# Linear attention into a bilinear feed-forward layer: an out product in three parts, sums moved and cut, a bank and a state copy moved

## The chip, the cores and the metric

One core of a Trainium2 chip runs the whole program in one launch. The metric is the device time of one execution in microseconds. It was 225.81 us before the change (median of 3 runs, 225.62 to 226.88).

## What is computed

Attention with a decay per head, in blocks with a running state, and then a bilinear feed-forward layer on its output:

```
for b in range(nb):                       # blocks along the sequence, S = 768
    intra = (q_b k_b^T * lam^(i-j), i >= j) v_b
    inter = (q_b * lam^(i+1)) kv_state
    out_b = intra + inter
    kv_state = lam^block * kv_state + (k_b * lam^(block-1-j))^T v_b
x   = out, heads side by side             # 3072 tokens x 512
out = ((x @ w_a) * (x @ w_b)) @ w_out     # d_ff = 1536, float32 in and out
```

There are 4 batches, 8 heads of 64 columns and 768 positions.

## The kernel before

The 3072 tokens are 24 units of 128 tokens, six to each batch. Eight groups of units, `GROUPS = (4, 1, 2, 4, 4, 4, 4, 1)`, go through the feed-forward layer one after the other, so unit 4 is group 1, units 5 and 6 are group 2, units 7 to 10 group 3, units 19 to 22 group 6 and unit 23 group 7.

TensorE always has the feed-forward layer of one group as its main work. The attention of later units is put between its matmuls by hand: the layer calls `hook(slot)` at numbered places, and `PLAN[group]` says which pieces stand at which slot. Each engine runs its own instructions in the order in which the program issues them. The pieces that matter here:

- `P u` (`PK` and `PV`): scale the keys and queries (GpSimd, line L401) and cast the values of unit u. From unit 7 on SP then starts a DMA that transposes keys and queries into `qkT` (L429); for units 4 to 6, `T u` does it on TensorE and ScalarE copies the result (L445).
- `S u`: the scores of unit u (TensorE, `kq`, L457) and their masks (`m`, VectorE, L480, for some units with a ScalarE copy ahead).
- `O2 (u, w)`: the outputs of two units (`o_ps`, L497), head half by head half; each half is copied by ScalarE into the transposed tile `xT` (L520) that the feed-forward layer reads. `V u` adds to the running state (`kvd`, L527) and copies it to `st`; `KV_ENG` says whether VectorE does this in one instruction (L560) or ScalarE in two (L558).
- `WS i`: one of eight sums of weight blocks, `wz_a` and `wz_b` (L269 to L275), by the engine in `WS_ENG`.
- `X g`: sums of `xT` for group g: `z_sub`, `z_add`, `z_mix` (L706 to L708).

Groups 0, 1, 2 and 7 go through `ffn`: for each of 12 column blocks `a_ps` (L596, copied by ScalarE, L605), `b_ps`, and their product `ab` (VectorE, L623); then the out product `op` (L643) and its copy by ScalarE (L634 or L638). For group 1 the out product has two halves of six matmuls, with slot 12 (`S 6`) between them and slot 13 (`P 8`, the outputs of units 5 and 6, `V 6`, both weight sums) behind them.

Groups 3 to 6 go through `ffn_z`, in which seven smaller products over sums of x and of weights stand for eight blocks. For each of 6 steps these go into banks called U, V and W (L731); ScalarE copies two of them out as `u` (L812) and VectorE subtracts those (`oab`, L760 to L777). The last product of a step waits for this and is issued in the next step; ScalarE then copies U (L737) and VectorE multiplies (L739). In the first step of group 3, which is not joined with an earlier group's out product, the order is: `xT` (U), first half of `z_sub` (V), first column half of `z_add` (W), `z_mix` (U), second column half of `z_add` (V), `xT` again (U); the second half of `z_sub` is read by the last product. The out products of groups 4 to 6 (L853) stand between the products of the following group; they too work with sums, of `ab` (`SM`), by VectorE or GpSimd.

PSUM has 7 banks in rotation. `ps_bank` hands out the next one that is not held; `z_bank` names U, V and W's banks itself. Before group 7 the last product of group 6 is issued into bank 1, and the rotation goes on from where it stood.

Of the kernel before, what the change touches and what calls it, by code (L numbers as in the profile page):

```python
# [17 lines left out]
BF16 = mybir.dt.bfloat16  # L18
# [4 lines left out]
def _bc(ap, dims):  # L23
# [58 lines left out]
Z_GROUPS = (3, 4, 5, 6)  # L82
# [10 lines left out]
                        [0] +  # L93
                        [1] +
                        [0] * 2))
KV_ENG = dict(enumerate(["dve"] * 10 + ["act"] * 2 + ["dve"] + ["act"] * 11))
VB_ENG = dict(enumerate(["pool"] * 7 +
                        ["dve"] * 3 +
                        ["pool"] * 5 +
# [5 lines left out]
                        ["act"] * 3))  # L105
SUM_ENG = {(3, 0): 'dve', (3, 1): 'dve', (3, 2): 'pool', (3, 3): 'dve', (3, 4): 'pool', (3, 5): 'pool', (3, 6): 'dve', (3, 7): 'dve', (4, 0): 'dve', (4, 1): 'pool', (4, 2): 'pool', (4, 3): 'pool', (4, 4): 'dve', (4, 5): 'pool', (4, 6): 'pool', (4, 7): 'pool', (5, 0): 'dve', (5, 1): 'dve', (5, 2): 'pool', (5, 3): 'pool', (5, 4): 'dve', (5, 5): 'pool', (5, 6): 'pool', (5, 7): 'dve', (6, 0): 'pool', (6, 1): 'dve', (6, 2): 'pool', (6, 3): 'dve', (6, 4): 'dve', (6, 5): 'pool', (6, 6): 'dve', (6, 7): 'dve'}
XS_ENG = {(3, 0): 'dve', (3, 1): 'dve', (3, 2): 'dve', (4, 0): 'dve', (4, 1): 'dve', (4, 2): 'dve', (5, 0): 'dve', (5, 1): 'pool', (5, 2): 'pool', (6, 0): 'pool', (6, 1): 'pool', (6, 2): 'pool'}
WS_ENG = {0: 'dve', 1: 'dve', 2: 'dve', 3: 'dve', 4: 'dve', 5: 'dve', 6: 'dve', 7: 'pool'}
WO_ENG = {0: 'dve', 1: 'dve', 2: 'pool', 3: 'dve', 4: 'dve'}
CO_ENG = {0: 'pool', 1: 'pool', 2: 'pool', 3: 'dve', 4: 'dve', 5: 'dve'}  # L110

# [2 lines left out]
def kernel(  # L114
# [11 lines left out]
    nc = tc.nc  # L126
    B, H, S, D = q.shape
# [3 lines left out]
    d_model, d_ff = moe_w_a.shape  # L131
# [4 lines left out]
    FC = d_ff // 128  # L136
# [10 lines left out]
    xz_pool = ctx.enter_context(tc.tile_pool(name="xz", bufs=4))  # L147
# [11 lines left out]
    bank = {"next": 0, "held": set(), "ffn": None}  # L159
# [169 lines left out]
    gx, xTs = {}, {}  # L329
# [67 lines left out]
    def eng_of(name):  # L397
        return nc.gpsimd if name == "pool" else nc.vector
# [232 lines left out]
    def store(row, op, lo, hi, queue=None):  # L631
        if row < g_u0[KEEP_GROUPS]:
            o_sb = snap_pool.tile([128, d_model], F32, name="o_kept", tag="snap")
            nc.scalar.copy(o_sb, op)  # L634
            kept.append((row, o_sb))
            return
        o_sb = o_pool.tile([128, d_model], F32, name="o_sb", tag="osb")
        nc.scalar.copy(o_sb[:, lo:hi], op[:, lo:hi])  # L638
        (queue or nc.sync).dma_start(out=out_r[row][:, lo:hi], in_=o_sb[:, lo:hi])

    def out_mms(op, ab, t, fs, lo=0, hi=d_model):
        for f in fs:
            nc.tensor.matmul(op[:, lo:hi], lhsT=ab[:, f, t * 128:(t + 1) * 128],  # L643
                             rhs=wo_sb[:, f, lo:hi], start=(f == 0), stop=(f == FC - 1))

    def ffn(u0, n, xT, hook, first, last):
        gt = n * BLK
        ab = ab_pool.tile([128, FC, 512], BF16, name="ab", tag="ab")
        if first:
            for i, cs in enumerate(W_STEPS):  # L650
                nxt = W_STEPS[i + 1] if i + 1 < len(W_STEPS) else ()
                fs = range(w_off[cs[0]] // 128, w_off[cs[-1] + 1] // 128)
                a_sbs = a_parts(fs[:2], xT, gt) if i == 0 else []
                a_sbs += [a_part(f, xT, gt) for f in fs[len(a_sbs):]]
                if i == 0:
                    kv_update(n0 - 1)
                    cast_w("b", cs[1], "both")
                else:
                    for c in nxt:
                        cast_w("a", c, "dve")  # L660
                for n_f, (f, a_sb) in enumerate(zip(fs, a_sbs)):
                    b_part(f, xT, gt, a_sb, ab)
                    hook(f)
                    if i == 0 and n_f == 1:
                        cast_w("a", nxt[0], "dve")
                for c in nxt:
                    cast_w("b", c, "act")
            ops = [ps_bank("op", [128, d_model], F32, hold=True) for _ in range(n)]
            slot = FC
            for c in range(FC // 2):  # L670
                for t in range(n):
                    out_mms(ops[t], ab, t, range(2 * c, 2 * c + 2))
                    if c == FC // 2 - 1:
                        store(u0 + t, ops[t], 0, d_model)
                    hook(slot)
                    slot += 1
            bank["held"].clear()
            return
        for f in range(FC):
            a_sb = a_part(f, xT, gt)  # L680
            b_part(f, xT, gt, a_sb, ab)
            hook(f)
        for t in range(n):
            op = ps_bank("op", [128, d_model], F32, ffn=True)
            if last and t == n - 1:
                for lo, hi in ((0, 256), (256, 384), (384, 512)):
                    if lo:
                        op = ps_bank("op", [128, d_model], F32, ffn=True)
                    out_mms(op, ab, t, range(FC), lo, hi)
                    store(u0 + t, op, lo, hi, nc.scalar if hi == d_model else None)  # L690
                return
            out_mms(op, ab, t, range(FC // 2))
            hook(FC + 2 * t)
            out_mms(op, ab, t, range(FC // 2, FC))
            store(u0 + t, op, 0, d_model)
            hook(FC + 2 * t + 1)


    xz = {}

    def x_sums(g):
        xT = gx[g]
        z_add = xz_pool.tile([128, 2, 512], BF16, name="z_add", tag="xz")
        z_sub = xz_pool.tile([128, KS, 256], BF16, name="z_sub", tag="xz")
        z_mix = mix_pool.tile([128, 2, 256], BF16, name="z_mix", tag="z_mix")
        eng_of(XS_ENG[g, 0]).tensor_sub(z_sub, xT[:, :, 0:256], xT[:, :, 256:512])  # L706
        eng_of(XS_ENG[g, 1]).tensor_add(z_add, xT[:, 0:2, :], xT[:, 2:4, :])
        eng_of(XS_ENG[g, 2]).tensor_add(z_mix, xT[:, 0:2, 0:256], xT[:, 2:4, 256:512])  # L708
        xz[g] = (z_add, z_sub, z_mix)

    fin = []
    pairs = [0]
# [285 lines left out]
    for g, n in enumerate(GROUPS):  # L998
        if g + 1 < len(GROUPS):
            new_xT(g + 1)  # L1000
        plan = {}
        for slot, name, us in PLAN.get(g, ()):
            plan.setdefault(slot, []).append((name, us))

        def hook(slot, plan=plan):
            for name, us in plan.get(slot, ()):
                if name == "C":
                    cast_w("o", us, CO_ENG[us])
                elif name == "PK":
                    prep_k(us)  # L1010
                elif name == "PV":
                    prep_v(us)
                elif name == "P":
                    prep_k(us)
                    prep_v(us)
                elif name == "W":
                    store_kept()
                elif name == "WS":
                    weight_sum(us)
                elif name == "WO":  # L1020
                    out_sum(us)
                elif name == "SM":
                    ab_sum(*us)
                elif name == "H":
                    out_half(*us)
                elif name == "X":
                    x_sums(us)
                elif name == "T":
                    piece_T(us)
                elif name == "S":  # L1030
                    piece_S(us)
                elif name == "VC":
                    kv_copy(us, kv["ps"], KV_ENG[us])
                elif name == "V":
                    piece_V(us)
                elif name == "O":
                    pieces_O((us,))
                elif name == "O2":
                    pieces_O(us)
                else:  # L1040
                    pieces_O(us[:2], us[2:])

        if g in Z_GROUPS:
            bank["held"] = set(range(5))
            joined = any(name == "H" and us[0] < g for slot, name, us in PLAN[g])
            own = any(slot >= 18 for slot, name, us in PLAN[g])
            ffn_z(g, g_u0[g], gx.pop(g), hook, joined, own)
        else:
            bank["held"] = {3, 4} if fin else set()
            if fin:  # L1050
                fin.pop()()
            ffn(g_u0[g], n, gx.pop(g), hook, g == 0, g + 1 == len(GROUPS))

# [28 lines left out]
```

## Time and profile before

| | |
|---|---|
| median of 3 runs | 225.81 us (225.62 to 226.88) |
| profiled execution | 225.77 us, of which 224.0 us are the span of the profile |
| TensorE busy | 213.6 us, 95% of the span |
| VectorE, ScalarE, GpSimd busy | 163.5, 123.4, 100.2 us |
| granted TensorE clock | 0.999 of full speed |

In a row of the timeline stand the start and the time taken in microseconds, the engine, the line, the operation, what is written and read, the shape and how many instructions are merged in the row; in brackets the idle time of the engine ahead of it and what ended it. PE is TensorE, PEld its weight loads, DVE VectorE, ACT ScalarE, POOL GpSimd, SP the engine that issues most DMAs. Some matmul records are missing, so a row that says x5 can stand for six. A matmul's end is modelled; its start is recorded.

### The profile page before, as it was taken

What the parts mean: (1) busy time and instruction counts of PE and PEld (TensorE: products, weight loads), DVE (VectorE), ACT (ScalarE), POOL (GpSimd) and SP (SyncE); (2) the same over time, 40 slices, a digit from 0 to 9 for tenths busy, and PEclk for the clock granted to TensorE, in tenths of its full rate; (3) what the DMA queues carried; (4) which work ended last, traced back from release to release, by engine and by line L of the source; (5) the groups of instructions that cost most, each with busy time, mean ns of one, the idle gap of its engine ahead of it and who ended that gap; (6) DMA issues with size and microseconds to landing.
All of it is one profiled execution on the core that took longest, in us unless ns stands there. A gap on an engine that the chain in (4) does not pass through costs nothing.

```text
span 224.0 us, 5599 instructions
## 1 busy us (share of the span) xinstructions
PE 213.6 (95%) x2225; PEld 159.0 (71%) x2235; DVE 163.5 (73%) x269; ACT 123.4 (55%) x251; POOL 100.2 (45%) x95
## 2 busy tenths in 40 slices
PE   7797999999999998999999999899999999999994
PEld 2374444448778756887547888688888888888994
DVE  0994763988798659889977979968686765776440
ACT  2684556018554156675366988776536665533322
POOL 6061004346794076542249369786427722052000
PEclk9999999999999999999999999999999999999999
DMA  4999999999999999999999999752021100112042
GB/s 128 322 253 349 357 387 340 272 221 208 218 187 220 233 188 245 190 281 231 154 247 219 224 220 230 145 94 50 0 96 47 51 0 4 47 52 91 0 143 94
DMA packets 99081, 39.42 MB, mean 176 GB/s; under 512 B 85488, under 2 KB 95088, under 8 KB 99056
## 3 DMA queue, kind: packets, MB, share of 16 engines
q1 hardware_dynamic: 98768, 39.00, 79.2%
q8 instruction: 17, 0.28, 0.6%
q10 hardware_dynamic: 288, 0.07, 0.1%
q14 instruction: 8, 0.07, 0.1%
HBM read 28.32 MB, written 6.29 MB: 154 GB/s over the span
## 4 chain that ended last, share of the span: by engine, by line
PE 86%; DMA 5%; SPq 3%; ACT 2%; DVE 2%; issue 1%; ACTq 0%
PE U L731 18%; PE op L853 12%; PE b_ps L596 10%; PE a_ps L596 9%; PE V L731 9%; PE op L643 9%; PE W L731 5%; PE op L793 5%; PE o_ps L497 4%; DMA wst<-in_moe_w_a_dram 3%; PE kq L457 3%; SPq L187 2%; DMA q<-in_q_dram 2%; PE kvd L527 1%; ACT xT L520 1%
## 5 line engine op out<-in xcount | busy, mean ns | idle before, releaser
L812 ACT COPY u<-U 128x512 f32<-128x512 f32 x48 | 28.4, 591 | 16.4 <-PE U L731 16.2
L401 POOL TENSOR_TENSOR qk<-kf,lp_k 128x512 bf16<-128x512 f32 x18 | 20.7, 1148 | 35.2 <-DMA kf<-in_k_dram 22.1
L623 DVE TENSOR_TENSOR ab<-a_sb,b_ps 128x128 bf16<-128x128 bf16 (+2 forms) x48 | 19.3, 417 | 16.4 <-PE b_ps L596 7.8
L596 PE MATMUL a_ps<-xT,wa_sb 128*128 128x128 bf16 (+2 forms) x198 | 27.6, 267 | 1.6 <-DVE wa_sb L244 1.3
L480 DVE TENSOR_TENSOR m<-kq,lotri 128x512 bf16<-128x512 f32 x40 | 25.7, 683 | 4.2 <-PE kq L457 4.2
L596 PE MATMUL b_ps<-xT,wb_sb 128*128 128x128 bf16 (+2 forms) x192 | 27.5, 272 | 0.5 <-ACT oab L737 0.5
L739 DVE TENSOR_TENSOR ab<-oab 128x1024 bf16<-128x1024 bf16 x24 | 18.4, 766 | 11.7 <-ACT oab L737 11.6
L605 ACT CAST a_sb<-a_ps 128x128 bf16<-128x128 f32 (+2 forms) x48 | 17.3, 375 | 16.7 <-PE a_ps L596 14.8
L401 POOL TENSOR_TENSOR qk<-qf,lp_q 128x512 bf16<-128x512 f32 x20 | 24.5, 1227 | 1.9 <-DMA qf<-in_q_dram 1.9
L643 PE MATMUL op<-wo_sb,ab 128*128 128x512 bf16 (+2 forms) x114 | 21.8, 334 | 0.5 <-issue 0.3
L596 PEld LDWEIGHTS <-wa_sb 128*128 128x128 bf16 x200 | 16.7, 98 | 7.7 <-DVE wa_sb L244 1.5
L731 PEld LDWEIGHTS <-wz_a 128*128 128x128 bf16 x192 | 18.2, 98 | 3.6 <-issue 0.5
L596 PEld LDWEIGHTS <-wb_sb 128*128 128x128 bf16 x192 | 15.7, 98 | 6.6 <-issue 0.6
L731 PEld LDWEIGHTS <-wz_b 128*128 128x128 bf16 x192 | 18.8, 98 | 2.2
L731 PE MATMUL U<-xT,wz_a 128*128 128x256 bf16 x96 | 18.3, 272 | 0.0
L731 PE MATMUL U<-xT,wz_b 128*128 128x256 bf16 x96 | 18.3, 272 | 0.0
L520 ACT CAST xT<-o_ps 128x512 bf16<-128x512 f32 (+1 forms) x24 | 12.2, 556 | 10.7 <-PE o_ps L497 10.5
L731 PEld LDWEIGHTS <-wa_sb 128*128 128x128 bf16 x144 | 13.4, 98 | 4.7 <-issue 2.0
L770 DVE TENSOR_TENSOR oab<-U,u 128x512 bf16<-128x512 f32 x24 | 16.4, 682 | 0.4 <-PE U L731 0.4
L643 PEld LDWEIGHTS <-ab 128*128 128x128 bf16 x120 | 10.2, 98 | 8.5
L737 ACT CAST oab<-U 128x512 bf16<-128x512 f32 x24 | 14.2, 591 | 3.5 <-PE U L731 3.5
L420 POOL CAST vb<-vf 128x512 bf16<-128x512 f32 x14 | 9.7, 695 | 13.4 <-DMA vf<-in_v_dram 12.5
(126 smaller groups left out, 451.9 us busy)
## 6 DMA issues: line engine op xcount, KB each, us to landing
vf<-in_v_dram SPq DMA_DIRECT2D x24, 256.0 KB, 5.1
qf<-in_q_dram SPq DMA_DIRECT2D x20, 256.0 KB, 4.5
kf<-in_k_dram SPq DMA_DIRECT2D x20, 256.0 KB, 4.7
out_dram<-o_sb SPq DMA_DIRECT2D x18, 256.0 KB, 2.4
wst<-in_moe_w_a_dram SPq DMA_DIRECT2D x6, 512.0 KB, 8.6
wst<-in_moe_w_b_dram SPq DMA_DIRECT2D x6, 512.0 KB, 9.1
wst<-in_moe_w_out_dram SPq DMA_DIRECT2D x6, 512.0 KB, 10.6
out_dram<-o_kept SPq DMA_DIRECT2D x5, 256.0 KB, 4.3
```

Of the source, the lines that this page charges most:

```text
L401: eng_of(eng).tensor_mul(dst.rearrange("p (c b) d -> p b c d", b=2), x[:].rearrange("p (b c) d -> p b c d", b=2), lp.rearrange("p (b c) o ...
L480: nc.vector.tensor_mul(m, kq[i], lotri_bc)
L520: nc.scalar.copy(dst, src)
L596: nc.tensor.matmul(ps[:, lo:hi], lhsT=w_sb[:, s, f * 128:(f + 1) * 128], rhs=xT[:, s, lo:hi], start=(s == 0), stop=(s == KS - 1), skip_gro ...
L605: nc.scalar.copy(a_sb[:, :gt], ps[:, :gt])
L623: nc.vector.tensor_mul(ab[:, f, :gt], a_sb[:, :gt], ps[:, :gt])
L643: nc.tensor.matmul(op[:, lo:hi], lhsT=ab[:, f, t * 128:(t + 1) * 128], rhs=wo_sb[:, f, lo:hi], start=(f == 0), stop=(f == FC - 1))
L731: nc.tensor.matmul(ps[:, k, :], lhsT=wt[:, s, n * 128:(n + 1) * 128], rhs=rhs[i][:, s, :], start=(fresh and k == 0 and s == 0), stop=True, ...
L739: nc.vector.tensor_mul(ab[:].rearrange("p (h i) (t c) -> p h i t c", h=2, t=2)[:, :, n], o5[:, :, :, 0, :], o5[:, :, :, 1, :])
L770: nc.vector.tensor_sub(oab[:, 1], U, v1)
L812: nc.scalar.copy(t, ps)
L853: nc.tensor.matmul(ps[:, t, :], lhsT=lhs[p][:, n, t * 128:(t + 1) * 128], rhs=rhs[:, n, :], start=fresh, stop=True, skip_group_check=True)
```

## The change

Five edits. Unit 4's out product is issued in three parts of four matmuls: slot 12 stands behind the first, slot 13 (with the outputs of units 5 and 6 and the state) behind the second, and the third part and the copy of `op` behind these. The last two weight sums move from slot 13 of group 1 to slots 7 and 9 of group 2, and sum 7 goes from GpSimd to VectorE. The sums of x for group 3 are cut from three instructions into five of 128 x 512, in the order in which the products read them; the first of them, over the first two units' columns, is issued ahead of the outputs of units 9 and 10. The state copy of unit 22 goes from ScalarE (two instructions) to VectorE (one). Group 7's rotation of banks starts at bank 5.

```diff
     1: [...
-        (11, 'S', 5), (11, 'T', 6), (12, 'S', 6), (13, 'P', 8), (13, 'O2', (5, 6)), (13, 'V', 6),
-        (13, 'WS', 6), (13, 'WS', 7)],
+        (11, 'S', 5), (11, 'T', 6), (12, 'S', 6), (13, 'P', 8), (13, 'O2', (5, 6)), (13, 'V', 6)],
     2: [(2, 'W', None), (2, 'W', None), (3, 'P', 9), (4, 'V', 7), (4, 'S', 7),
-        (6, 'V', 8), (10, 'PK', 10), (11, 'PV', 10), (11, 'P', 11), (11, 'W', None),
+        (6, 'V', 8), (7, 'WS', 6), (9, 'WS', 7), (10, 'PK', 10), (11, 'PV', 10), (11, 'P', 11), (11, 'W', None),
         (11, 'S', 8), (11, 'P', 12), (12, 'Q', (7, 8, 9, 10)), (13, 'P', 13),
-        (13, 'W', None), (13, 'V', 9), (14, 'O2', (9, 10)), (14, 'X', 3), (15, 'W', None)],
+        (13, 'W', None), (13, 'V', 9), (14, 'XA', 3), (14, 'O2', (9, 10)), (14, 'X', 3), (15, 'W', None)],
...
-KV_ENG = dict(enumerate(["dve"] * 10 + ["act"] * 2 + ["dve"] + ["act"] * 11))
+KV_ENG = dict(enumerate(["dve"] * 10 + ["act"] * 2 + ["dve"] + ["act"] * 9 + ["dve", "act"]))
...
-WS_ENG = {..., 7: 'pool'}
+WS_ENG = {..., 7: 'dve'}
...
+            if n == 1:
+                out_mms(op, ab, t, range(4))
+                hook(FC)
+                out_mms(op, ab, t, range(4, 8))
+                hook(FC + 1)
+                out_mms(op, ab, t, range(8, FC))
+                store(u0 + t, op, 0, d_model)
+                return
...
+    def x_add_first(g):
+        x_first[g] = x_tile()
+        nc.vector.tensor_add(x_first[g][:, :, 0:256], gx[g][:, 0:2, 0:256], gx[g][:, 2:4, 0:256])
...
+        z_add = x_first.pop(g) if g in x_first else x_tile()
+        add_half = lambda c: nc.vector.tensor_add(z_add[:, :, c], xT[:, 0:2, c], xT[:, 2:4, c])
...
+        if g == Z_GROUPS[0]:
+            sub = lambda s: nc.vector.tensor_sub(z_sub[:, s], xT[:, s, 0:256], xT[:, s, 256:512])
+            sub(slice(0, 2))
+            nc.vector.tensor_add(z_mix, xT[:, 0:2, 0:256], xT[:, 2:4, 256:512])
+            add_half(slice(256, 512))
+            sub(slice(2, 4))
+            return
...
+                elif name == "XA":
+                    x_add_first(us)
...
             bank["held"] = {3, 4} if fin else set()
             if fin:
+                bank["next"] = 5
                 fin.pop()()
             ffn(g_u0[g], n, gx.pop(g), hook, g == 0, g + 1 == len(GROUPS))
```

More of the change, by code (lines that the diff above doesn't have):

```diff
@@ L107 @@
 XS_ENG = {(3, 0): 'dve', (3, 1): 'dve', (3, 2): 'dve', (4, 0): 'dve', (4, 1): 'dve', (4, 2): 'dve', (5, 0): 'dve', (5, 1): 'pool', (5, 2): 'pool', (6, 0): 'pool', (6, 1): 'pool', (6, 2): 'pool'}
-WS_ENG = {0: 'dve', 1: 'dve', 2: 'dve', 3: 'dve', 4: 'dve', 5: 'dve', 6: 'dve', 7: 'pool'}
+WS_ENG = {0: 'dve', 1: 'dve', 2: 'dve', 3: 'dve', 4: 'dve', 5: 'dve', 6: 'dve', 7: 'dve'}
 WO_ENG = {0: 'dve', 1: 'dve', 2: 'pool', 3: 'dve', 4: 'dve'}
@@ L699, with x_tile @@
     xz = {}
+    x_first = {}
+    def x_tile():
+        return xz_pool.tile([128, 2, 512], BF16, name="z_add", tag="xz")
+    def x_add_first(g):
+        x_first[g] = x_tile()
+        nc.vector.tensor_add(x_first[g][:, :, 0:256], gx[g][:, 0:2, 0:256], gx[g][:, 2:4, 0:256])
     def x_sums(g):
         xT = gx[g]
-        z_add = xz_pool.tile([128, 2, 512], BF16, name="z_add", tag="xz")
+        z_add = x_first.pop(g) if g in x_first else x_tile()
+        add_half = lambda c: nc.vector.tensor_add(z_add[:, :, c], xT[:, 0:2, c], xT[:, 2:4, c])
         z_sub = xz_pool.tile([128, KS, 256], BF16, name="z_sub", tag="xz")
         z_mix = mix_pool.tile([128, 2, 256], BF16, name="z_mix", tag="z_mix")
+        xz[g] = (z_add, z_sub, z_mix)
+        if g == Z_GROUPS[0]:
[5 more added lines that the diff above has]
+            return
         eng_of(XS_ENG[g, 0]).tensor_sub(z_sub, xT[:, :, 0:256], xT[:, :, 256:512])
@@ L708, in x_sums @@
         eng_of(XS_ENG[g, 2]).tensor_add(z_mix, xT[:, 0:2, 0:256], xT[:, 2:4, 256:512])
-        xz[g] = (z_add, z_sub, z_mix)
     fin = []
```

## The prediction

> **What bounds the kernel now.** I read the page first, then the list of waits of TensorE, then the timeline around each place that the diff touches. The page:
>
> ```profile
> span 224.0 us, 5599 instructions
> PE 213.6 (95%) x2225; PEld 159.0 (71%) x2235; DVE 163.5 (73%) x269; ACT 123.4 (55%) x251; POOL 100.2 (45%) x95
> ```
>
> TensorE is busy for 213.6 of 224.0 us, so the kernel ends when TensorE's queue ends, and a change can only pay by closing one of its holes. The change removes no matmul. The profiled execution took 225.77 us, 1.77 more than its span; the median of the runs is 225.81, so I subtract from 225.77 and compare with 225.81. The list of waits shows late in the kernel
>
> ```profile
> PE b_ps L596 <- ACT oab L737: 0.5, 1, 0.5
> ```
>
> but a modelled matmul end reaches into the hole behind it, so I measure holes from start to start. The pitch comes from the third timeline below: two matmuls of 256 columns start at 84.67, the next two at 84.89, so 0.11 us each; by columns 0.055 for 128 and 0.22 for 512.
>
> **Unit 4's out product.** The timeline of the stretch:
>
> ```profile
> 59.21 1.46 PE L643 MATMUL op<-wo_sb,ab 128*128 128x512 bf16 x5
> 59.41 1.01 ACT L445 COPY qkT<-tps 128x1024 bf16<-128x1024 bf16 x1 [0.84 <-PE tps L443]
> ...
> 60.60 0.40 PE L457 MATMUL kq<-qkT 64*128 64x128 bf16 x8
> ...
> 60.93 1.47 PE L643 MATMUL op<-wo_sb,ab 128*128 128x512 bf16 x6
> 61.03 1.29 DVE L480 TENSOR_TENSOR m<-kq,lotri 128x512 bf16<-128x512 f32 x2 [0.89 <-PE kq L457]
> 61.21 3.09 POOL L275 TENSOR_TENSOR wz_b<-wb_sb 128x1536 bf16<-128x1536 bf16 x1
> ...
> 62.43 0.59 ACT L634 COPY o_kept<-op 128x512 f32<-128x512 f32 x1 [2.01 <-PE op L643]
> ...
> 62.56 0.64 PE L497 MATMUL o_ps<-m,vb 128*64 128x128 bf16 x16
> 63.02 1.07 ACT L520 CAST xT<-o_ps 128x512 bf16<-128x512 f32 x2
> 63.13 0.40 PE L527 MATMUL kvd<-vb,qk 128*128 128x128 bf16 x4
> ...
> 63.65 0.87 PE L596 MATMUL a_ps<-xT,wa_sb 128*128 128x256 bf16 x4
> ...
> 64.36 0.60 PE L596 MATMUL b_ps<-xT,wb_sb 128*128 128x256 bf16 x4
> ```
>
> Before, ScalarE copies `op` (62.43) and only then the xT of units 5 and 6 (to 64.09). Unstalled, four kvd matmuls from 63.13 end at 63.35 and four a_ps matmuls at 63.79; b_ps starts at 64.36. Hole: 0.57 us.
>
> After, four of the twelve matmuls (0.87 us) stand behind kvd, and the copy of `op` behind the xT copies. What is late next lies earlier: with four matmuls instead of six ahead of unit 6's scores, these could start 0.07 behind them as before, at 59.21 + 0.87 + 0.07 = 60.15, but the qkT copy ends at 59.41 + 1.01 = 60.42, so about 60.5: a new hole of 0.3. Scores take 0.33, four `op` matmuls end at 61.7. The masks come 0.1 earlier than before, ending at 62.2; the second half of o_ps needs them, runs from 62.27 to 62.5, kvd from 62.6 to 62.82, the last four `op` matmuls to 63.7. xT is copied by 63.4 and hides under them. b_ps then starts at 63.7 + 0.44 = 64.13. Gain 0.23; I take 0.2. Best end 0.35, if the qkT wait is shorter; worst end -0.1, because the second a_ps group uses `op`'s bank, whose copy now ends about 64.3 while that group wants it at 64.57.
>
> **The two weight sums.** GpSimd loses 3.09 us at 61.21 and VectorE gets it as a second sum, both later in group 2. Of VectorE's own earlier sum, and of its waits between 60 and 90 us:
>
> ```profile
> L273 DVE TENSOR_TENSOR wz_b<-wb_sb,wz_b x1: 984/984/984, 53.6 to 53.6; 128x1536 bf16<-128x1536 bf16 x1
> ...
> DVE ab L623 <- PE b_ps L596: 2.2, 5, 0.5
> ```
>
> Two sums are 1.97 us; behind them in VectorE's queue stand the `ab` products of f = 8 to 11 and unit 8's masks. VectorE waits 2.2 us for b_ps in this group, four of the five waits at its end, where the sums now stand, so this is the cover and the cost is zero. With that cover gone the masks, and the o_ps of units 7 and 8 with them, would be up to 1 us late. wz is first read in group 3, 8 us later. No DMA moves: SP's order is the same.
>
> **The sums of x for group 3.** TensorE, then the engines that feed it:
>
> ```profile
> 84.06 0.38 PE L731 MATMUL U<-xT,wz_b 128*128 128x256 bf16 x2
> 84.67 0.38 PE L731 MATMUL V<-z_sub,wa_sb 128*128 128x256 bf16 x2 [0.23 <-DVE z_sub L706]
> 84.89 0.38 PE L731 MATMUL V<-z_sub,wb_sb 128*128 128x256 bf16 x2
> 85.68 0.38 PE L731 MATMUL W<-z_add,wa_sb 128*128 128x256 bf16 x2 [0.42 <-DVE z_add L707]
> ...
> 89.61 0.38 PE L731 MATMUL U<-z_sub,wa_sb 128*128 128x256 bf16 x2
> ...
> 82.30 1.07 ACT L520 CAST xT<-o_ps 128x512 bf16<-128x512 f32 x2 [1.63 <-PE o_ps L497]
> ...
> 83.40 1.21 DVE L706 TENSOR_TENSOR z_sub<-xT 128x1024 bf16<-128x1024 bf16 x1 [2.40 <-ACT xT L520]
> 84.54 1.09 DVE L707 TENSOR_TENSOR z_add<-xT 128x1024 bf16<-128x1024 bf16 x1
> 85.56 0.41 DVE L708 TENSOR_TENSOR z_mix<-xT 128x512 bf16<-128x512 bf16 x1
> ...
> 88.45 0.68 DVE L770 TENSOR_TENSOR oab<-U,u 128x512 bf16<-128x512 f32 x1
> ...
> 83.03 1.04 POOL L401 TENSOR_TENSOR qk<-qf,lp_q 128x512 bf16<-128x512 f32 x1
> 84.01 1.07 POOL L420 CAST vb<-vf 128x512 bf16<-128x512 f32 x1
> ```
>
> V was due at 84.28 (hole 0.39), W at 85.11 (hole 0.57): 0.96 us. After, the first half of z_add is made before the last outputs, in idle time, and the first half of z_sub needs only the first xT copy (82.86). z_sub at 83.40 ends just after GpSimd's instruction of 83.03 to 84.07, and the cast behind that is stretched: the two engines take turns. With turns taken, in the times of before: z_sub's first half waits until GpSimd changes instructions at 83.07 and ends 83.45, GpSimd's next 84.5, z_mix 84.85, the cast 85.5, the second half of z_add 85.85, the rest of z_sub 86.2. TensorE asks at 84.28 (V), 84.72 (W), 85.15 (z_mix) and 86.04 (second z_add): none late. But VectorE's queue behind the sums does not come earlier: its `oab` of 88.45 ends near 88.7 instead of 89.13, and the product of 89.61 is now due at 88.65. I take off 0.1: gain 0.86, between 0.45 (one of the parts late by half a microsecond) and 0.96.
>
> The pieces carry a fixed cost: 512 elements take 0.41. The Trainium skill (VectorE: DVE Perf Modes, section on the TRN2 errata) speaks against such cuts: it charges a fixed cost per instruction, which many small tiles pay each time, and advises 512 elements or more. These have 512. By its formula a piece is (58 + 256) / 0.96 = 327 ns as an estimate, and the row here decides with 410.
>
> **The state copy of unit 22 and the bank of group 7.** Two timelines:
>
> ```profile
> 169.69 0.75 ACT L558 CAST st<-kvd 64x256 bf16<-64x256 f32 x2
> ...
> 170.57 0.38 PE L731 MATMUL V<-z_sub,wb_sb 128*128 128x256 bf16 x2
> ...
> 171.10 0.38 PE L731 MATMUL U<-z_mix,wz_a 128*128 128x256 bf16 x2
> ...
> 174.49 1.47 POOL L708 TENSOR_TENSOR z_mix<-xT 128x512 bf16<-128x512 bf16 x1
> ...
> 176.15 0.38 PE L731 MATMUL U<-z_mix,wz_a 128*128 128x256 bf16 x2
> ```
>
> The U of 171.10 was due at 170.79 (0.31) and waits for ScalarE's copy of U, queued behind two state copies (0.75). With these on VectorE it goes. But GpSimd's z_mix for group 6 ends at 175.96 and U at 176.15 reads it; GpSimd does not come earlier, so only 0.15 is kept (0 to 0.31).
>
> ```profile
> 203.09 0.39 PE L596 MATMUL a_ps<-xT,wa_sb 128*128 128x128 bf16 x4
> ...
> 203.96 0.69 DVE L739 TENSOR_TENSOR ab<-oab 128x1024 bf16<-128x1024 bf16 x1 [0.49 <-ACT oab L737]
> 203.97 0.38 PE L596 MATMUL b_ps<-xT,wb_sb 128*128 128x128 bf16 x4 [0.49 <-ACT oab L737]
> ```
>
> b_ps was due at 203.31: 0.66. It takes bank 1, from which ScalarE still copies U; starting at bank 5 gives it bank 6, free since unit 23's outputs. Next late: unit 19's second half product needs the `ab` that ends at 204.65 and comes to it at 204.63. Gain 0.58 (0.45 to 0.66).
>
> **Sum:** 0.2 + 0.86 + 0.15 + 0.58 = 1.79; 225.77 - 1.79 = **224.0 us**. Best ends: 0.35 + 0.96 + 0.31 + 0.66 = 2.28, 223.5. Worst: -0.1 + 0.45 + 0 + 0.45 = 0.8, 225.0.
>
> **Rivals.** *The port.* VectorE loses every turn: z_mix comes only after GpSimd's cast as well, about 85.5, z_add's half 85.9, and the rest 86.3; TensorE waits 0.4 at z_mix and 0.3 more at `oab`. The third gain falls to 0.25: 224.6. For it speaks z_sub's 1.21; against it the stretched cast. The Trainium skill (SBUF — State Buffer, section on the two separate sides) calls the shared pair of ports an exclusive lock held for the whole instruction. By that rule each part may wait a whole GpSimd instruction; the trace agrees in the 1.21 against 0.41 for half the elements.
>
> *The transposes, slower.* Keys and queries come transposed by DMA, in SP's fixed order, and TensorE now asks earlier:
>
> ```profile
> 85.49 1.42 SPq L429 DMA_TRANSPOSE qkT<-qk  x1
> ...
> 91.02 0.40 PE L457 MATMUL kq<-qkT 64*128 64x128 bf16 x8
> ...
> DMA to landing us min/median/max: 3.0/4.5/6.9
> ```
>
> Unit 12's transpose, at the median, lands at 90.0, and 89.8 with the first 0.2 of gain; its scores are now wanted at 91.02 - 1.06 = 89.96. At the maximum it lands at 92.4, 1.4 later than the scores started before; with the later 0.73 regained that is 226.4. From a landing of 6.3 us on it costs more than the change gives. Against it: unit 12's own scores started unstalled. A landing of about 5 us would cost half a microsecond: 224.5.
>
> *The cut is empty.* If the waits for qkT and the masks eat the first gain wholly: 224.2, inside the range.
>
> **How the numbers follow.** The forecast with its bounds has 0.72, the port 0.10, a transpose late by 0.3 to 1.2 us 0.10 (224.3 to 225.2), a transpose late by more 0.06, the rest 0.02. A measurement of this kernel tells about 0.5% from no change, that is 1.13 us: faster is below 224.68. Nearly all of the forecast (0.68), most of the port (0.07) and a third of the mild transposes (0.03) lie there: 0.78. Slower has 0.06, the same 0.16. The range from 223.4 to 225.2 takes in the bounds, the port and the mild transposes.
>
> **What would show it.** TensorE's b_ps after unit 6's kvd about 0.2 earlier, with a wait of 0.3 ahead of unit 6's scores; no hole ahead of the first V and W of group 3; VectorE's two sums near 73 and 75 us without a late mask; the U near 171 without a hole, but a new one at z_mix near 176; b_ps of group 7 right behind a_ps. Wrong would be a wait of kq for qkT in group 3, or holes in group 3's first two steps that sum to over 0.5.

## The result and the profile after

The changed kernel takes 224.50 us (median of 20 runs, 223.47 to 227.21), the kernel before 225.75 us (20 runs, 224.32 to 231.45). The ratio is 0.9954, interval 0.9936 to 0.9973. So it is faster, by about 1.0 us by the ratio and 1.25 by the medians; the forecast was 1.8. The profiled execution took 224.95 us, 0.8 less than that of before. A ratio leaves out runs that stand out as disturbed (of e9 below three of twelve, 227.9 to 229.5 us), so here and below it need not be the quotient of the medians.

The page of the kernel after: TensorE is still busy for 95% of the span.

```profile
span 223.2 us, 5600 instructions
PE 213.1 (95%) x2225; PEld 158.9 (71%) x2235; DVE 164.5 (74%) x273; ACT 122.6 (55%) x249; POOL 95.8 (43%) x94
```

Its list of TensorE's waits (total, times, longest, in us). The wait of `b_ps` for ScalarE's `oab`, shown of before, is gone. The first line here is new and is now the longest of all:

```profile
PE V L755 <- ACT u L836: 1.5, 1, 1.5
...
PE kq L456 <- ACT qkT L444: 0.2, 1, 0.2
```

Lines of the kernel after are shifted: the products are L755 (L731 before), the `u` copies L836 (L812), stores of kept outputs L628 (L629), scores L456, `a_ps` and `b_ps` L595. In what follows, a lead is how much earlier a matmul starts than the same matmul in the profiled run of before.

The timeline around unit 4's out product. Scores of unit 6 wait for ScalarE's qkT copy, then `a_ps` and `b_ps` follow without a hole (63.43 - 63.00 is four matmuls at 0.11):

```profile
58.73 1.01 ACT L444 COPY qkT<-tps 128x1024 bf16<-128x1024 bf16 x1 [0.84 <-PE tps L442]
...
59.80 0.40 PE L456 MATMUL kq<-qkT 64*128 64x128 bf16 x8 [0.24 <-ACT qkT L444]
...
62.13 1.03 PE L642 MATMUL op<-wo_sb,ab 128*128 128x512 bf16 x4
...
63.00 0.60 PE L595 MATMUL a_ps<-xT,wa_sb 128*128 128x256 bf16 x4
...
63.43 0.60 PE L595 MATMUL b_ps<-xT,wb_sb 128*128 128x256 bf16 x4
```

VectorE's weight sums in group 2, and the masks behind them, which start as soon as VectorE is free:

```profile
71.92 0.94 DVE L274 TENSOR_TENSOR wz_a<-wa_sb 128x1536 bf16<-128x1536 bf16 x1
...
73.45 0.94 DVE L274 TENSOR_TENSOR wz_b<-wb_sb 128x1536 bf16<-128x1536 bf16 x1
...
74.98 1.27 DVE L479 TENSOR_TENSOR m<-kq,lotri 128x512 bf16<-128x512 f32 x2
```

The first two steps of group 3. V and W start without a hole. Then TensorE stops between 88.17 and 89.86:

```profile
81.99 0.42 DVE L725 TENSOR_TENSOR z_sub<-xT 128x512 bf16<-128x512 bf16 x1 [1.18 <-ACT xT L519]
...
82.65 1.16 POOL L400 TENSOR_TENSOR qk<-kf,lp_k 128x512 bf16<-128x512 f32 x1 [2.11 <-DMA kf<-in_k_dram]
82.82 1.26 DVE L720 TENSOR_TENSOR z_add<-xT 128x512 bf16<-128x512 bf16 x1
...
83.36 0.38 PE L755 MATMUL V<-z_sub,wa_sb 128*128 128x256 bf16 x2
...
83.79 0.38 PE L755 MATMUL W<-z_add,wa_sb 128*128 128x256 bf16 x2
...
84.47 1.51 SPq L628 DMA_DIRECT2D out_dram<-o_kept  x1
...
87.95 0.38 PE L755 MATMUL U<-z_sub,wb_sb 128*128 128x256 bf16 x2
...
89.22 0.58 ACT L836 COPY u<-V 128x512 f32<-128x512 f32 x1 [2.01 <-DMA out_dram<-o_kept]
...
89.86 0.38 PE L755 MATMUL V<-z_add,wz_a 128*128 128x256 bf16 x2 [1.52 <-ACT u L836]
```

The chain of waits of the kernel after in this stretch (start, time taken, what) goes through SP's queue and a store, where that of before went through the sums of x:

```profile
79.93 0.62 POOL vb L419
80.55 1.72 SPq L428
...
83.56 0.87 SPq L186
...
84.47 4.67 DMA out_dram<-o_kept
...
89.22 0.59 ACT u L836
```

What happens: ScalarE's second `u` copy of step 2 writes into a rotation of seven buffers, `snap`, and takes the one that held the out product of unit 2. That output leaves by a store in SP's queue, behind unit 11's transpose (80.01) and unit 13's three loads, and the buffer is free when the store has landed, at 84.47 + 4.67 = 89.14. In the kernel before the same pair is there, and hidden by a hair. Its timeline, and the store in its list of DMA issues (KB, median us to landing):

```profile
84.19 1.19 SPq L629 DMA_DIRECT2D out_dram<-o_kept  x1
...
88.98 0.59 ACT L812 COPY u<-V 128x512 f32<-128x512 f32 x1
out_dram<-o_kept SPq DMA_DIRECT2D x1, 256.0 KB, 4.5
```

Landed at 88.7, copy at 88.98: 0.3 us to spare, and TensorE now comes over a microsecond and a half earlier, while the store comes 0.3 later. The next transfer is no better off. Unit 12's transpose, issued at 86.09, landed 4.0 us later, at 90.1, and its scores stand here:

```profile
86.09 1.41 SPq L428 DMA_TRANSPOSE qkT<-qk  x1
...
90.87 0.40 PE L456 MATMUL kq<-qkT 64*128 64x128 bf16 x8
```

They did not wait for it; without the hole of 1.69 ahead of them they would have been due at 89.18, 0.9 us ahead of that landing (an estimate from these rows).

Late in the kernel after, the U near 171 follows V directly; one step later V waits instead, for VectorE's `oab`, which reads the bank that V takes and ends at 175.42; and `b_ps` of group 7 stands right behind `a_ps`:

```profile
170.71 0.38 PE L755 MATMUL U<-z_mix,wz_a 128*128 128x256 bf16 x2
...
173.71 1.10 DVE L854 TENSOR_TENSOR zab<-ab 128x768 bf16<-128x768 bf16 x1
...
174.36 1.47 POOL L733 TENSOR_TENSOR z_mix<-xT 128x512 bf16<-128x512 bf16 x1
...
174.74 0.68 DVE L801 TENSOR_TENSOR oab<-W,u 128x512 bf16<-128x512 f32 x1
...
175.47 0.39 PE L755 MATMUL V<-z_sub,wa_sb 128*128 128x256 bf16 x2
...
202.87 0.39 PE L595 MATMUL a_ps<-xT,wa_sb 128*128 128x128 bf16 x4
203.09 0.39 PE L595 MATMUL b_ps<-xT,wb_sb 128*128 128x128 bf16 x4
```

The `zab` ahead of that `oab` took 1.10 us here and 0.85 in the kernel before. U, which reads `z_mix`, follows V without a hole at 175.92, 0.09 behind the end of `z_mix`.

TensorE's lead, step by step, in the two profiled runs:

| at | lead before and behind it, us | forecast gain |
|---|---|---|
| first `a_ps`, 17.53; by 54.3 | 1.59; 0.67 (ahead of every edit) | none |
| `b_ps` of 63.43 | 0.67 to 0.93 | 0.2 |
| V and W of 83.36, 83.79 | 0.93 to 1.89 | 0.86 |
| V of 89.86, the store | 1.89 to 0.19 | not seen |
| U of 170.71, V of 175.47 | 0.08 to 0.39, then 0.23 | 0.15 |
| `b_ps` of 203.09, end | 0.23 to 0.88, then 0.79 | 0.58 |

Of the 0.79 at the end, 0.67 was there ahead of every edit, and the store took more than that away in between. So this pair of runs alone does not show the gain; the 20 runs of each kernel do.

### The profile page after: what moved, and what is told of

It is laid out like the page before. It is cut to its first block, busy times and chain, and to the rows that moved or that the text cites. A ratio compares the mean times of both kernels' runs of the same rounds, so it can differ in the third digit from the quotient of the medians.

```text
span 223.2 us, 5600 instructions
## 1 busy us (share of the span) xinstructions
PE 213.1 (95%) x2225; PEld 158.9 (71%) x2235; DVE 164.5 (74%) x273; ACT 122.6 (55%) x249; POOL 95.8 (43%) x94
## 4 chain that ended last, share of the span: by engine, by line
PE 67%; DMA 13%; SPq 9%; DVE 4%; issue 2%; ACT 2%; POOL 1%; ACTq 0%; DVEq 0%; POOLq 0%
PE U L755 16%; PE op L877 12%; PE V L755 9%; PE b_ps L595 6%; PE a_ps L595 6%; DMA kf<-in_k_dram 5%; PE op L817 5%; PE W L755 4%; SPq L186 4%; DMA wst<-in_moe_w_b_dram 4%; SPq L227 3%; PE o_ps L496 3%; PE op L642 2%; DMA q<-in_q_dram 2%; PE kq L456 2%
## 5 line engine op out<-in xcount | busy, mean ns | idle before, releaser
L836 ACT COPY u<-U 128x512 f32<-128x512 f32 x48 | 28.3, 590 | 16.5 <-PE U L755 16.4
L400 POOL TENSOR_TENSOR qk<-kf,lp_k 128x512 bf16<-128x512 f32 x18 | 19.7, 1093 | 37.9 <-DMA kf<-in_k_dram 28.7
L595 PE MATMUL b_ps<-xT,wb_sb 128*128 128x128 bf16 (+2 forms) x192 | 27.5, 272 | 0.5 <-DVE ab L622 0.5
L595 PE MATMUL a_ps<-xT,wa_sb 128*128 128x128 bf16 (+2 forms) x198 | 27.3, 267 | 0.1
L400 POOL TENSOR_TENSOR qk<-qf,lp_q 128x512 bf16<-128x512 f32 x20 | 23.7, 1186 | 1.8 <-DMA qf<-in_q_dram 1.8
L755 PEld LDWEIGHTS <-wz_a 128*128 128x128 bf16 x192 | 18.2, 98 | 5.1 <-issue 2.0
L595 PEld LDWEIGHTS <-wa_sb 128*128 128x128 bf16 x200 | 16.7, 98 | 5.8 <-DVE wa_sb L253 0.2
L595 PEld LDWEIGHTS <-wb_sb 128*128 128x128 bf16 x192 | 15.8, 98 | 6.5 <-issue 0.6
L755 PEld LDWEIGHTS <-wz_b 128*128 128x128 bf16 x192 | 18.7, 98 | 2.2
L755 PE MATMUL U<-xT,wz_a 128*128 128x256 bf16 x96 | 18.3, 272 | 0.0
L755 PE MATMUL U<-xT,wz_b 128*128 128x256 bf16 x96 | 18.3, 272 | 0.0
L419 POOL CAST vb<-vf 128x512 bf16<-128x512 f32 x14 | 10.2, 726 | 15.2 <-DMA vf<-in_v_dram 15.2
L836 ACT COPY u<-V 128x512 f32<-128x512 f32 x24 | 14.2, 594 | 4.3 <-PE V L755 2.1
L755 PEld LDWEIGHTS <-wa_sb 128*128 128x128 bf16 x144 | 13.4, 98 | 4.0 <-issue 1.0
```

What stands on the lines that cost most here:

```text
L400: eng_of(eng).tensor_mul(dst.rearrange("p (c b) d -> p b c d", b=2), x[:].rearrange("p (b c) d -> p b c d", b=2), lp.rearrange("p (b c) o ...
L595: nc.tensor.matmul(ps[:, lo:hi], lhsT=w_sb[:, s, f * 128:(f + 1) * 128], rhs=xT[:, s, lo:hi], start=(s == 0), stop=(s == KS - 1), skip_gro ...
L755: nc.tensor.matmul(ps[:, k, :], lhsT=wt[:, s, n * 128:(n + 1) * 128], rhs=rhs[i][:, s, :], start=(fresh and k == 0 and s == 0), stop=True, ...
L836: nc.scalar.copy(t, ps)
```

## The experiments

Two theories. **The DMA queue**: from 50 to 140 us SP's transfers follow each other in a fixed order, and they, not TensorE's work, set a time below which TensorE can't get there; whichever transfer is next late takes a gain back. **One slot**: only this store is badly placed, and with it moved the gain of the sums arrives. A third possibility is that the sums gain nothing of their own. Each kernel was profiled once, so a hole named below is that of one execution.

Each kernel's median is compared with the kernel before on the same chip. "No cut" leaves the sums of x for group 3 in three instructions.

| | kernel | median, before, us | ratio, 95% |
|---|---|---|---|
| e1 | after, store earlier | 224.51, 225.42 | 0.9946 (0.9916 to 0.9976) |
| e2 | after, no cut | 224.73, 225.42 | 0.9973 (0.9939 to 1.0007) |
| e3 | before, store earlier | 225.43, 225.42 | 1.0002 (0.9978 to 1.0026) |
| e4 | e1, no cut | 225.35, 225.42 | 0.9986 (0.9958 to 1.0014) |
| e5 | after, own buffers | 224.27, 225.55 | 0.9944 (0.9914 to 0.9974) |
| e6 | before, own buffers | 225.80, 225.55 | 1.0014 (0.9988 to 1.0041) |
| e7 | e5, no cut | 224.59, 225.55 | 0.9962 (0.9930 to 0.9994) |
| e8 | before, bank only | 225.16, 225.55 | 0.9967 (0.9938 to 0.9997) |
| e9 | e5, stores in group 3 | 225.72, 226.24 | 0.9957 (0.9928 to 0.9987) |
| e10 | e9, no cut | 225.39, 226.24 | 0.9989 (0.9957 to 1.0021) |
| e11 | before, three parts and weight sums only | 226.43, 226.24 | 1.0000 (0.9968 to 1.0032) |
| e12 | e5, stores in group 4 | 227.99, 225.67 | 1.0103 (1.0052 to 1.0154) |

**The store earlier, with and without the cut (e1 to e4).** In e1, and likewise in e3 on the kernel before and in e4 on e2:

```diff
-... (11, 'P', 11), (11, 'W', None),
+... (11, 'W', None), (11, 'P', 11),
```

> The changed kernel, with one slot entry swapped: the store of unit 2's kept rows is issued ahead of unit 11's transpose and unit 13's loads instead of behind them. Theory S (store): in the changed kernel ScalarE's copy of V in the second step of group 3 waits for that store to land, since the copy takes the store's buffer, and the gain of group 3's first step is lost there. Then the hole of 1.7 us ahead of the second z_add product of that step goes, the first step's gain of about 0.9 us is kept, and the time falls 0.5 to 1.0 us below the changed kernel, to a ratio of about 0.991 against the kernel before. If the next DMA, unit 12's transpose, takes the store's place, a hole ahead of unit 12's scores of up to 1 us shows instead. Rival E (engines): the hole comes from VectorE or ScalarE being busy; then it stays, and the ratio stays at 0.995.

e2 leaves the first half of `z_add` out of slot 14 and goes back to three sums:

```diff
-        (13, 'W', None), (13, 'V', 9), (14, 'XA', 3), (14, 'O2', (9, 10)), (14, 'X', 3), ...
+        (13, 'W', None), (13, 'V', 9), (14, 'O2', (9, 10)), (14, 'X', 3), ...
...
-        if g == Z_GROUPS[0]:
+        if False:
```

> The changed kernel without the cut of the sums of x (three instructions again, none ahead of the last outputs). Theory S: the two holes of 0.4 and 0.6 us ahead of V and W come back, but the hole at the kept store shrinks by as much, so the time is within 0.3 us of the changed kernel: ratio about 0.995 to 0.996. Rival E: the cut is worth its 0.9 us, and the ratio rises to 0.999.

> The kernel before, with the store of unit 2's kept rows issued earlier, as in the first run. Theory S: before the change the store landed at 88.71 and the copy that needs its buffer began at 88.98 without a wait, so it gains little: ratio 0.998 to 1.000 (a run whose start is quicker than that of the profile would gain by it). Rival E: no change, 1.000.

> The changed kernel with the early store and without the cut of the sums of x. Theory S: with the store out of the way the cut shows its worth, so this is 0.6 to 0.9 us slower than the run with the early store and the cut; ratio about 0.995. Rival E: the same as the changed kernel without the cut, 0.999.

In e1 unit 2's store lands at 83.5 and the hole at 88 is gone. Two others take its place. The timeline of e1:

```profile
85.16 0.40 PE L456 MATMUL kq<-qkT 64*128 64x128 bf16 x8 [0.41 <-DMA qkT<-qk]
...
100.09 0.58 ACT L836 COPY u<-U 128x512 f32<-128x512 f32 x1 [1.19 <-DMA out_dram<-o_kept]
...
100.73 0.38 PE L755 MATMUL U<-xT,wz_a 128*128 128x256 bf16 x2 [0.38 <-ACT u L836]
```

The first is the transpose of unit 11, which now stands behind the store; the second is unit 3's store. They cost 0.57 (0.09 of it is there in the kernel before) and 0.54 from start to start, and the lead goes from 1.99 at W to 0.96 at 100.7 us. That is against the one slot. e2's list of waits shows that the old holes are back and the store's is not:

```profile
PE W L755 <- DVE z_add L732: 0.4, 1, 0.4
```

In e2 V and W wait 0.18 and 0.58, the store lands at 88.04, and the lead is 1.09 both at 63.3 and at 88.5 us. So in the profiled runs the cut gained 0.96 and the store took 1.69 in one kernel, and the other had neither; e2's span is 222.5 us, not longer than that of after. By their ratios the cut is worth 0.2% without e1's edit and 0.4% with it, with an interval of 0.3% to either side on each ratio. e4 was expected near 0.995 and came out at 0.9986; in its profiled run the uncut sums left holes of 0.57 at V, 1.02 at W and 0.32 at `z_mix`, in sum twice those of the kernel before. e3 moves the same store in the kernel before and changes nothing, as it should where the store is hidden.

**Buffers of their own (e5 to e7).** The kept outputs of units 2 to 4 go into memory that nothing uses between the loading of weights and group 4's sums, so no `u` copy waits for them:

```diff
-            o_sb = snap_pool.tile([128, d_model], F32, name="o_kept", tag="snap")
+            if row < 2:
+                o_sb = snap_pool.tile([128, d_model], F32, name="o_kept", tag="snap")
+            else:
+                if not kept_own:
+                    kept_own.append(sum_tile([128, 3, d_model], F32, "o_kept", "zab"))
+                o_sb = kept_own[0][:, row - 2]
```

> The changed kernel, with the kept outputs of units 2, 3 and 4 in memory of their own (that of the sums of ab, unused until group 4) instead of buffers that ScalarE's copies u take over; the order of all instructions stays. Theory S (the store sets a floor): no copy of u waits for a kept store, the hole of 1.7 us is gone without moving any DMA, and the gain of the cut sums stays: 0.5 to 1.0 us below the changed kernel, ratio 0.990 to 0.993. Theory D (the DMA chain as a whole sets the floor, the store is only its first member): kq in group 3 then waits for a transposed qkT, with holes of 0.3 to 1 us, and the ratio is 0.993 to 0.996. Rival E (an engine): the hole stays at 1.7.

> The kernel before with the same memory of their own for the kept outputs. Theory S and D: the store had 0.3 us of slack in the profile, so between no change and 0.4 us faster, where a run starts its first matmuls early: ratio 0.998 to 1.000.

> The changed kernel with that memory for the kept outputs, and without the cut of the sums of x. Theory S: 0.7 to 1.0 us slower than with the cut, ratio about 0.995 to 0.997. Theory D: within 0.4 us of it. Rival E: 0.999.

The wait for the stores is gone in e5, and the next transfer is late: unit 12's transpose. The timeline of e5:

```profile
90.60 0.40 PE L456 MATMUL kq<-qkT 64*128 64x128 bf16 x8 [0.53 <-DMA qkT<-qk]
```

0.69 us from start to start; the lead falls from 1.03 at W to 0.42 here. In e7, without the cut, unit 12's scores do not wait, and in e6 nothing is gained. The ratios of e5 and e7 differ by 0.2%. Freeing the buffer moved the wait to the next transfer and no further.

**The bank alone (e8).**

```diff
             if fin:
+                bank["next"] = 5
                 fin.pop()()
```

> The kernel before with the bank edit alone (group 7's rotation starts at bank 5). All theories: the hole of 0.66 us ahead of group 7's first b_ps goes and 0.58 of it stays gained, since nothing but TensorE's queue follows: ratio 0.997 to 0.998.

```profile
203.75 0.39 PE L596 MATMUL a_ps<-xT,wa_sb 128*128 128x128 bf16 x4
203.97 0.39 PE L596 MATMUL b_ps<-xT,wb_sb 128*128 128x128 bf16 x4
```

The hole of 0.66 is gone here too, in the kernel before with this one line. From 132.25 on e8 was 0.66 us behind the run of before; it came out of `b_ps` level and is 0.09 behind at 205.6. So 0.57 are kept. The ratio, 0.33%, is 0.74 us, in its interval 0.07 to 1.4.

**The stores out of the way (e9, e10, e12).** With e5's buffers the three stores can be issued later. e9 moves them to slot 16 of group 3, e10 is e9 without the cut:

```diff
-        (6, 'V', 8), ... (11, 'P', 11), (11, 'W', None),
+        (6, 'V', 8), ... (11, 'P', 11),
...
-        (13, 'W', None), (13, 'V', 9), (14, 'XA', 3), ..., (15, 'W', None)],
+        (13, 'V', 9), (14, 'XA', 3), ...],
...
+        (15, 'P', 15), (16, 'W', None), (16, 'W', None), (16, 'W', None), (17, 'WO', 0), ...
```

> The changed kernel with memory of their own for the kept outputs of units 2, 3 and 4, and their three stores (0.77 MB) moved from group 2 to slot 16 of group 3, behind the loads for unit 17, so that unit 12's and 13's transposes and loads stand three stores earlier in SP's queue. Theory D (the DMA chain sets a floor for TensorE near 91 us, through whichever transfer lands last): unit 12's transpose lands 1 us or more earlier, near 89, the hole of 0.7 us ahead of unit 12's scores goes, and 0.3 to 0.7 us more of the cut's gain stays: ratio 0.990 to 0.993. Rival F (the floor lies elsewhere, in the loads of values or later): new holes of the same sum, ratio 0.994 to 0.996.

> As the run before, without the cut of the sums of x. Theory D: with the DMA chain out of the way the cut is worth most of its 0.9 us, so this is 0.5 to 0.9 us slower than with it. Rival F: within 0.3 us.

In e9 no hole is left between 84 and 104 us but those of before, and the lead, 0.65 at 63.7 and 1.61 at W, is still 1.55 at 100 us. Then ScalarE's copy of an out product, 10 us behind the last of the stores, waits for a buffer whose own store comes late. From ScalarE's and TensorE's lists of waits of e9, and SP's timeline:

```profile
ACT o_sb L643 <- DMA out_dram<-o_sb: 5.1, 1, 5.1
...
PE U L761 <- ACT u L842: 2.5, 1, 2.5
...
107.50 2.36 SPq L629 DMA_DIRECT2D out_dram<-o_kept  x3
```

2.68 us from start to start at 121.17: more than was gained. In e10 the sums are in the way as before (W waits 0.7, `z_mix` 0.6), TensorE is 1.44 behind e9 at 105 us, and the same copy holds nobody at 121 (a hole of 0.37, behind VectorE's `oab`, stands at 131.9). By the ratios e9 is 0.3% faster than e10 all the same, but over all twelve runs of each its median, 225.72, is above e10's 225.39. Its profiled run took 226.30 us; how long the others stopped at 121 is not known, so this pair does not settle what the cut is worth.

e12 puts the stores where SP's queue was empty in e9, ahead of unit 21's transpose:

```diff
-        (13, 'P', 21), (16, 'SM', (4, 0)), ...
+        (13, 'W', None), (13, 'W', None), (13, 'W', None), (13, 'P', 21), (16, 'SM', (4, 0)), ...
```

> Changed: the kernel after, with the kept outputs of units 2 to 4 in memory of their own, and their three stores issued in group 4, slot 13, behind the loads of unit 22 and ahead of the transpose of unit 21. In the kernel that issues them in group 3, slot 16, SP's queue has nothing to issue there from 136.6 to 141.6 us, and TensorE kept its whole lead from the sums of x (0.65 us ahead of the kernel before at 63.7, 1.61 at 84.1, 1.54 at 100.1), until ScalarE's copy of an out product waited 5.11 us for a store that stood behind the three. Theory that the DMA queue takes the gain back: with no store added between 80 and 135 us no hole over 0.3 us is new from 84 to 140 us, the sums' 0.96 is still there at 170, and the sum at the end is 0.2 + 0.96 + 0.15 + 0.57 = 1.9 us beyond what the start gives: ratio about 0.992, below 0.9935. Rival, that something other than these stores and transposes holds TensorE to a time in group 3 or 4 (the sums on VectorE and GpSimd, ScalarE's queue): a new hole of 0.7 to 1 us somewhere from 85 to 140 all the same, with no DMA as its releaser, and a ratio of 0.9955 like the kernel after. Against both: VectorE's first sum of the out product of group 4, due at 142.4, waits for the three stores in that memory; then a new hole near 143 to 156 us.

The kernel is 1% slower, by the case that the text above puts against both theories; yet up to there it is the clearest run. In e12 the lead is 1.66 at W, 1.60 at 100 us and 1.54 at 139.7. The last matmul ahead of the stop, its counterpart in the kernel before (the second row), and what stopped it in e12:

```profile
139.72 0.38 PE L761 MATMUL U<-xT,wz_b 128*128 128x256 bf16 x2
141.26 0.38 PE L731 MATMUL U<-xT,wz_b 128*128 128x256 bf16 x2
142.19 0.56 DVE L856 TENSOR_TENSOR zab<-ab 128x768 bf16<-128x768 bf16 x1 [2.41 <-DMA out_dram<-o_kept]
143.41 0.58 PE L761 MATMUL U<-z_sub,wa_sb 128*128 128x256 bf16 x2 [3.31 <-DVE oab L800]
```

With none of these stores between 80 and 135 us the 0.97 of the sums is carried for 56 us, with a loss of 0.1. The rival, another limit in groups 3 and 4, is refuted for this run. At 140 the first sum of group 4 wants the memory that the stores still hold, and 2.5 us are lost beyond the hole of before; some more goes to the clock (last section). The memory was chosen badly: stores landing 2.4 us earlier, or memory that nothing wants at 140, were not tried, so a version that keeps the whole gain to the end was not shown. e1, e5 and the kernel after can't be told apart.

**Three parts and weight sums alone (e11).**

```diff
+            if n == 1:
+                out_mms(op, ab, t, range(4))
+                hook(FC)
...
-        (13, 'WS', 6), (13, 'WS', 7)],
...
+        (6, 'V', 8), (7, 'WS', 6), (9, 'WS', 7), ...
...
-WS_ENG = {..., 7: 'pool'}
+WS_ENG = {..., 7: 'dve'}
```

> The kernel before with the first two edits alone: unit 4's out product in three parts and the two weight sums later, by VectorE. By the prediction's working: a new hole of 0.3 us ahead of unit 6's scores, none ahead of group 2's first a_ps and b_ps, 0.2 us gained there; of that between nothing and 0.2 us reaches the end: ratio 0.999 to 1.000. Rival: the sums on VectorE hold the products up, and a hole of 0.5 us or more shows in group 2.

The timeline of e11: the same wait ahead of unit 6's scores, and `b_ps` 0.43 behind `a_ps` without a hole.

```profile
61.19 0.40 PE L456 MATMUL kq<-qkT 64*128 64x128 bf16 x8 [0.24 <-ACT qkT L444]
...
64.39 0.60 PE L595 MATMUL a_ps<-xT,wa_sb 128*128 128x256 bf16 x4
64.82 0.60 PE L595 MATMUL b_ps<-xT,wb_sb 128*128 128x256 bf16 x4
```

This run was 0.72 behind that of before at 55.7 and is 0.46 behind at 64.8: 0.26 gained. Then the uncut sums meet GpSimd at a worse moment; its list of waits has

```profile
PE W L738 <- DVE z_add L714: 0.9, 1, 0.9
```

where before had 0.42, and with V and `z_mix` the holes there sum to 0.69 + 1.01 + 0.32 = 2.02 against 0.97: more than the 0.26 is lost again, in this run. `z_sub` and `z_add` took 1.51 and 1.52 us beside GpSimd here, 1.21 and 1.09 in the kernel before. In e2, which has the same two edits, V and W waited only 0.18 and 0.58, so these holes differ from run to run. In the nine profiled runs with uncut sums they add up to between 0.76 (e2) and 2.0 us (e11); in the five with the cut there is none. The ratio of 1.0000 says no gain, with 0.7 us to either side.

## Why the prediction was right, and where not

The sign, the time (224.5 in 223.4 to 225.2) and the reason, holes of TensorE closed, were right; the gain, 1.0 us by the ratio, is little over half of the 1.79 forecast. By its steps:

**Unit 4's out product**: forecast 0.2, with a new wait of 0.3 ahead of unit 6's scores. The wait is there (0.24 by the list, 0.31 from start to start), no hole is left at `b_ps`, and 0.24 to 0.27 were gained in all ten profiled runs that have the edit. **The weight sums**: forecast nothing. The two sums of 0.94 are hidden, and the masks at 74.98 hold nobody.

**The sums of x** is the term that was mis-sized. Its own account was good: holes at V and W of 0.96 closed, gained 0.96, no part late. (That the hole was 0.96 hung on the run: without the cut it was 0.76 to 2.0.) But "gain 0.86" was meant to reach the end. In the profiled run 1.69 were lost five microseconds later, more than this term; over four pairs of kernels, each with and without the cut, the ratios differ by 0.19, 0.40, 0.18 and 0.32%, on the mean 0.27% or 0.6 us (0.26% without e9 and e10), with intervals of up to 0.3% on each ratio, so no pair alone gives the size. The step that failed is the search for what is late next. It went down VectorE's queue, to `oab` at 88.7, and took 0.1 off; it did not go down ScalarE's, where the `u` copy 0.3 us behind a store's landing was in the trace. e1, e5 and e9 show that this store is one of several, and e12 that with none of them in the way the term keeps its size, up to 140 us.

**The rival of the transposes** had the mechanism: SP's fixed order against a TensorE that asks earlier. It named one transfer, unit 12's, and put its landing between on time and 1.4 us behind the old start of the scores. In the kernel after the transfer was a store in the same queue, and unit 12's scores did not wait, though by the estimate above they were the next in line; in e5, with the store out of the way, they waited just 0.69, close to the mild case. "A wait of kq for qkT in group 3" was the wrong sign to look for, "holes in group 3's first two steps that sum to over 0.5" the right one: 1.69. The chance of 0.16 for late transposes was too small, for it counted one transfer of the queue and not its neighbours.

**The port**: VectorE and GpSimd did stretch each other (the second `z_add` piece took 1.26 beside GpSimd's 1.16, a `z_sub` piece of the same size 0.42 alone), and still no piece was late. **The state copy**: 0.31 gained at 171, 0.16 lost one step later, 0.15 kept. The size is the forecast's; the wait is not. V of 175.47 waited for VectorE's `oab`, and the U that reads `z_mix` did not wait. With V on time U would have been due at 175.76, just ahead of the end of `z_mix` at 175.83, so the forecast wait was close; that the sum came out even so is luck. **The bank**: forecast 0.58; 0.65 at `b_ps` and 0.56 behind the next wait, and 0.57 in e8.

That the time still came within half a microsecond of 224.0 owes much to the bank: its one line alone measured 0.33% (e8) where all five edits measured 0.46%, within wide intervals. It and the state copy lie behind the last load, where no transfer takes a gain back.

## What to carry to other kernels

When a change lets the busiest engine come earlier in a stretch where the DMA queue is full, go through the queue's next few microseconds transfer by transfer, stores too, and set each landing beside the first instruction that needs its data or its buffer. A store is a load of free space: in a rotation of buffers somebody waits for its landing, and a slack of 0.3 us in the trace of before bounds what is kept past that place, unless the transfer comes earlier too: here 0.19 was left of a lead of 1.89.

## What the runs showed of the hardware

**A head start is kept in some runs and lost in others.** The first `a_ps` started between 17.5 and 19.1 us in these runs, though no edit lies ahead of it; the run of before is among the last. Of the lead over it, seven runs had lost 0.4 to 1.6 us by 56 us, still ahead of the five edits, and the others, apart from e6, which had none, at most 0.1. In the kernel after most of the loss is one wait, of `b_ps` at 54.30 for VectorE's `ab` behind two weight sums. These took 1.36 and 1.35 us there, and 0.95 and 0.98 in the run of before. What sets it in the other runs was not followed up. So leads of two single runs are compared here from place to place, and not at the end alone.

**Half the clock after a long stop.** TensorE's stop in e12 was 3.5 us from start to start. The windows of e12 (TensorE, its weight loads, VectorE, ScalarE, GpSimd busy, then the granted clock, DMA share and GB/s):

```profile
139.00:143.00 4.00, 1.10 (x15) 0.63 (x13) 1.50 (x3) 1.20 (x3) 0.17 (x1) 0.96 1.13 194
143.00:145.00 2.00, 1.59 (x8) 1.13 (x8) 2.00 (x4) 0.50 (x1) 2.00 (x2) 0.50 1.19 239
145.00:147.00 2.00, 2.00 (x17) 1.55 (x16) 2.00 (x3) 1.25 (x3) 1.78 (x2) 0.72 0.59 99
147.00:150.00 3.00, 3.00 (x60) 2.49 (x58) 1.62 (x3) 2.06 (x5) 2.51 (x2) 1.00 0.47 87
```

Behind the stop each pair of matmuls of 256 columns starts 0.43 us behind the pair before, where it is 0.22 otherwise, and the lead falls by another 1.3 us, from -0.95 at 143.41 to -2.27 at 146.68. The stops of 2.7 us in e9 and 1.7 in the kernel after left the clock at 1.00. The Trainium skill (TensorE: Matmul & The Clock Gate, section Part 1: The HAM clock gate) says that TensorE falls back to half its clock after an idle window of about 3.4 us; these three stops agree. It puts the way back at a busy window of the same length; here the pitch was whole again at 146.1, 2.7 us behind the stop, and the measurement decides. So this stop cost 1.3 us more than its own length.
